# A spectral filter and a GEGLU block in one kernel: full rows in a product's last pass, signs moved from the filter to the row copies, shorter column steps

## The chip, the cores and the metric

The kernel runs on one core of a Trainium2 chip. It is measured by the device time of one execution in microseconds; the median over several executions counts, and less is better. The engines are TensorE (PE, with PEld for the loading of its weights), VectorE (DVE), ScalarE (ACT), GpSimd (POOL) and SyncE (SP). In this kernel GpSimd and SyncE do nearly nothing but issue DMAs.

## What is computed

Two branches work on the same 2048 x 576 input in fp32, and a sigmoid gate for each row mixes them:

```python
def reference(A_x, A_w_r, A_w_i, B_x, B_w_gate, B_w_up, B_w_down, gate_w):
    x = A_x                                              # [1, 2048, 576]
    g = sigmoid((x * gate_w).sum(-1, keepdims=True))
    a = irfft2(rfft2(x) * (A_w_r + 1j * A_w_i))          # spectral branch
    h = gelu(x @ B_w_gate) * (x @ B_w_up)                # 576 -> 4608
    b = h @ B_w_down                                     # 4608 -> 576
    return g * a + (1 - g) * b
```

## The kernel before

**GEGLU on TensorE.** An fp32 operand is split into a high and a low part that TensorE multiplies at its fast fp32 rate, and a product of two is the sum high x high, high x low, low x high. The 18 blocks of 256 hidden features are worked once for each half of 1024 rows. The first two blocks run plainly (`chain`); the other 34 turns are *products* (`products`, numbered from 0; product 16 is the first with the second half's rows). A product multiplies the first 512 input features in Strassen's manner: seven combinations of weights (`Block.prep`) by seven of the rows (named a11, a12, s2, s3, s1, a22, s4). `Block.seven` issues one such multiplication for 128 hidden features: six matmuls over 128 rows at L1367 and, at L1369, a last pass for the 64 remaining input features. Two sevens for each combination make 14 in a product. Behind them come the *downs* (12 matmuls at L966 in `down_mm`), whose result ScalarE scales into `stg` (L998) and GpSimd adds to the DRAM rows `yd` (`put`, L979, an accumulating DMA).

**The tails.** The 64 remaining features are worked in halves of 32. Their weights are made ready by `tail_piece`, ten pieces in all: load `wt` (L1245), form the seven combinations (`total`, L1249), take the high part, take the rest, and store them to `tails_d` in DRAM (L1263), as three groups of rows: high, high, low. Two pieces are handled during the plain blocks, eight in the first products, one every 12 gaps; all use the same buffer `wtb`. For every slot of weights `prep` then loads 96 rows of it (L1346, through SyncE). The row operand beside them, made by `tail_of`, has 128 rows: high, low, high, low; the last pass reads 96 of them.

**The spectral branch** runs between: the row transform on VectorE and ScalarE, the column transform, the product with the filter, and back. `columns` does the column transform for 16 blocks `kb` of frequencies; each takes two products of six matmuls on TensorE (L350) with matrices `col` (loaded by GpSimd, L336) and a pair of filter tiles `wf` (loaded by SyncE, L340). Frequencies past 288 are held as the conjugates of others, so the imaginary part of the filter takes a sign there (`sgn`, a multiplication at L439 for each block). `moved` copies the rows into the layout of the column stage and back, real parts on ScalarE, imaginary parts on VectorE (L570). At the end `adds` multiplies the spectral rows by the gate and GpSimd adds them to `yd` (L713). The last downs take the last eight blocks of rows from `yd` again (`load_last`, L1020, through SyncE), add theirs on VectorE (L1031) and write the output.

**What sets the order.** The program is written in one order, and each engine takes its instructions in that order. After each seven and each down stands a `gap()`: it runs functions that were put off by `at(n, fn)` to the n-th gap from there, and then lets the generator of the spectral branch go on for as long as `credit` lasts, which matmuls fill (`tick`) and work on VectorE uses up. A `yield None` in the generator ends the gap; `waits(n)` ends n. One block of `columns` takes 9 gaps at least (`STEP`).

**Between the halves.** The second half's operands are made in `other_operands` (called by `spectral`): ScalarE's copies (`highs`, through L234, the one line of all copies), VectorE's differences (`rests`, L1171, and `sums`, L1103), and stores to `kept` in DRAM. In product 15, the last of the first half, `swap` loads them into the operands (L1092 and L1093, on GpSimd's queue) as each becomes free: this is the *switch*, and the wait for the new operands falls in product 16. `forward` and `backward` are the butterflies over blocks of columns; `beside` runs them as a second generator next to the blocks.

Of the kernel before, what the change touches and what calls it, by code (L numbers as in the profile page):

```python
# [29 lines left out]
RATE = 1.08  # L30
STEP = 9
FIRST = 2
# [127 lines left out]
def _build(nc, tc, a):  # L160
    with ExitStack() as ctx:
# [34 lines left out]
        def set_tmp():  # L196
# [17 lines left out]
                for n in ("a11", "a12", "s2", "s3", "s1", "a22", "s4")}  # L214
        tails_d = [dram.tile([3 * P, 7 * 256], F32, name=f"tails{i}", tag=f"tails{i}") for i in range(len(PAIRS))]
        yd = [dram.tile([P, D], F32, name=f"yd{i}", tag=f"yd{i}") for i in range(NB)]
# [16 lines left out]
        def copy(o, i):  # L233
            act.activation(o, i, AF.Copy)  # L234
# [53 lines left out]
        def columns():  # L288
            G = [[rows[:, SW * (4 * i + j):SW * (4 * i + j + 1)] for j in range(4)] for i in range(2)]
            signs = rows[:, 8 * SW:8 * SW + KF]  # L290
            z, vs, w0 = (wtb[:, SW * i:SW * (i + 1)] for i in range(3))
            tmps = [free_low[:, SW * i:SW * (i + 1)] for i in range(2)]
            w1 = zb[0][:, 1664:1664 + SW]
            t0 = zb[0][:, 1664 + SW:1664 + SW + NK]
            turn = [d + 4 * q for d in range(4) for q in range(4)]
# [83 lines left out]

            def beside():  # L380
                yield from forward(1)
                for d in range(2):
                    yield from backward(d)
                    yield from forward(d + 2)
                for d in range(2, 4):
                    yield from backward(d)
# [7 lines left out]
            load_g(0)  # L394
            yield from waits(3)
            colm = mk("tmp", [2 * UNIT + 104], F32R)
# [7 lines left out]
            for c in range(2):  # L404
                load_ww(0, c)
            nc.sync.dma_start(signs, a["sgn"])
            at(2, lambda: load_g(1))
# [10 lines left out]
            for kb in range(16):  # L418
# [19 lines left out]
                vec.tensor_tensor(z, z, w0, ALU.mult)  # L438
                vec.tensor_tensor(two(w1)[:, :, 0:KF], two(w1)[:, :, 0:KF], signs[:, None, :].to_broadcast([P, 2, KF]), ALU.mult)  # L439
                yield from step(1.52)  # L440
                vec.tensor_tensor(vs, vs, w1, ALU.mult)
                vec.tensor_tensor(z, z, vs, ALU.add)
                yield from step(1.52)
                vec.tensor_tensor(vs2[:, 0], zr, zi, ALU.add)
# [12 lines left out]
                yield from waits(STEP - 9)  # L457
            copy(yh, vs)
# [105 lines left out]
        def moved(at, ts):  # L564

            for t in ts:
                for c in range(2):
                    o, i = at(t, c)
                    if c:
                        vec.tensor_copy(o, i)  # L570
# [578 lines left out]
        def other_operands():  # L1149
# [42 lines left out]

            yield from waits(4)
            load_xs(1, 2, quads[2])
# [46 lines left out]
        def tail_piece(n, raw_t=raw_t, high_t=high_t):  # L1241
# [17 lines left out]
            def store():  # L1259
                d = tails_d[n // 2].rearrange("(r p) (m c k) -> r p c m k", r=3, m=7, c=2)  # L1260
                w = 32 * len(PAIRS[n // 2])
                for r, x in enumerate((f(high_t), f(high_t), raw_t)):
                    nc.sync.dma_start(d[r, 0:w, n % 2], x[0:w])  # L1263
                stored[n // 2] = n % 2
# [3 lines left out]
        class Block:  # L1268
# [57 lines left out]
            def prep(self, k, m, lead=0):  # L1326
# [15 lines left out]
                def tail():  # L1342
                    n, q = self.tail_at[self.groups[k][1]]
                    assert stored[n]
                    d = tails_d[n].rearrange("(r q p) k -> q r p k", r=3, q=4)
                    nc.sync.dma_start(f(w[0:96, 512:768]), d[q, :, :, 256 * m:256 * (m + 1)])  # L1346

# [12 lines left out]
            def seven(self, ps, k, m, x, s, first, soon=None):  # L1360
# [3 lines left out]
                for t in range(2):  # L1364
                    hi, lo = (w[:, n + P * s:n + P * (s + 1)] for n in ((256, 0), (768, 1024))[t])
                    for q, (l, x) in enumerate(((hi, xh), (lo, xh), (hi, xl))):
                        pe.matmul(ps, l, x[:, t], start=first and t == 0 and q == 0, stop=False,  # L1367
                                  skip_group_check=True)
                pe.matmul(ps, w[0:96, 512 + P * s:512 + P * (s + 1)], xt[0:96], start=False, stop=True,  # L1369
                          skip_group_check=True)  # L1370
# [5 lines left out]
        def products(b, k):  # L1376
# [38 lines left out]
            for n, (name, nd) in enumerate(zip(("a11", "a12", "s2", "s3", "s1", "a22", "s4"), downs)):  # L1415
# [24 lines left out]
                for s in range(2):  # L1440
# [230 lines left out]
```

## Time and profile before

| | |
|---|---|
| runs | 1366.65, 1367.49 (median), 1371.56 us |
| profiled execution | 1365.51 us, of it the span 1363.4 us |
| mean granted TensorE clock | 0.991 |
| data moved by DMA | 262.71 MB, mean 193 GB/s |
| of it GpSimd's queue | 100.69 MB |
| of it SyncE's queue | 160.28 MB |

The chain of work that ended last is TensorE for 69%, DMA for 12%, issuing for 9%, ScalarE for 4%. Its largest parts by line are the downs (L966, 23%) and the sevens (L1367, 35%). Times in the rows below are microseconds from the span's start; a bracket behind a row gives the idle time of the engine before it and what ended it, and `x2` that two instructions of the same form follow each other. SPq and POOLq are the queues in which SyncE and GpSimd issue DMAs.

### The profile page before, as it was taken

The numbers are of one execution on the slowest core, as the hardware profiler recorded it, in microseconds if no ns is written. First come the engines' busy times: TensorE is split into PE (matmuls) and PEld (weight loads), VectorE is DVE, ScalarE is ACT, GpSimd is POOL, SyncE is SP. The second block draws the span as 40 slices with busy tenths as digits, with TensorE's granted clock in tenths as the row PEclk, the third lists the DMA queues.
The fourth block names the chain that finished last, engine by engine and source line by source line (L and its number), as shares of the span: only waits on it lengthen the run. The fifth ranks groups of instructions, "written<-read, shape, count | busy, mean of one in ns | idle before, by whom it ended". The sixth has DMA issues, their size and how long they took to land.

```text
span 1363.4 us, 20503 instructions
## 1 busy us (share of the span) xinstructions
PE 1322.1 (97%) x7210; PEld 1159.4 (85%) x7210; DVE 1137.4 (83%) x1750; ACT 841.8 (62%) x1419; POOL 283.7 (21%) x360
## 2 busy tenths in 40 slices
PE   9999999999999988999889999999999999999996
PEld 7888888888888877788778888888888888888896
DVE  8889889879999967587858778876899996799975
ACT  6665655666555656777557876766655656656551
POOL 0011211211221111224420122221221223222132
PEclk9999999999999999999989999999999999999999
DMA  9669998797767899979996698798877779867789
GB/s 350 211 159 218 198 228 188 166 248 143 134 134 136 193 295 257 240 160 269 329 220 174 174 245 174 156 215 188 168 134 137 133 135 201 199 124 132 128 181 233
DMA packets 165025, 262.71 MB, mean 193 GB/s; under 512 B 14394, under 2 KB 79226, under 8 KB 164026
## 3 DMA queue, kind: packets, MB, share of 16 engines
q0 software_dynamic: 50000, 100.69, 45.9%
q1 hardware_dynamic: 114490, 160.28, 36.6%
q8 instruction: 56, 0.92, 0.3%
q10 hardware_dynamic: 432, 0.44, 0.1%
q14 instruction: 47, 0.39, 0.1%
HBM read 140.64 MB, written 122.48 MB: 193 GB/s over the span
## 4 chain that ended last, share of the span: by engine, by line
PE 69%; DMA 12%; issue 9%; ACT 4%; DVE 3%; POOL 2%; SPq 0%; POOLq 0%; DVEq 0%; ACTq 0%
PE pdn L966 23%; PE pgu L1367 18%; PE px L1367 17%; PE pgu L1369 3%; PE px L1369 3%; POOL yd L979 2%; PE pdn L350 2%; DMA gub<-tails 2%; DMA kept_a<-tmp 2%; DMA slot<-tails 2%; DMA low<-ws 2%; DMA yd<-wtb 1%; DMA rows<-away 1%; ACT stg L998 1%; DMA tails<-wtb 1%
## 5 line engine op out<-in xcount | busy, mean ns | idle before, releaser
L979 POOL DMA_DIRECT2D yd<-stg x264 | 227.4, 864 | 998.3 <-ACT stg L998 871.1
L998 ACT ACTIVATE stg<-pdn,omg 128x576 f32<-128x576 f32 x276 | 204.6, 742 | 343.7 <-PE pdn L966 214.2
L966 PE MATMUL pdn<-dn,hb 128*128 128x288 f32 x1356 | 202.5, 296 | 3.0 <-ACT stg L998 2.7
L966 PEld LDWEIGHTS pdn<-dn,hb 128*128 128x128 f32 x1356 | 193.8, 189 | 12.7 <-ACT stg L998 3.9
L1367 PE MATMUL pgu<-xhi,gub 128*128 128x512 f32 x480 | 151.6, 397 | 4.3 <-ACT px L234 4.3
L966 PEld LDWEIGHTS pdn<-dn,ext 128*128 128x128 f32 x816 | 123.2, 189 | 15.0 <-DVE low L1031 4.8
L966 PE MATMUL pdn<-dn,ext 128*128 128x288 f32 x816 | 130.9, 296 | 4.4 <-DVE low L1031 4.4
L1367 PE MATMUL pgu<-til,gub 128*128 128x512 f32 x516 | 133.6, 394 | 1.4 <-ACT xraw L234 1.0
L966 PE MATMUL pdn<-dn,gub 128*128 128x288 f32 x816 | 129.3, 294 | 0.0
L234 ACT ACTIVATE gub<-low 128x512 fp32r<-128x512 f32 (+1 forms) x163 | 100.9, 620 | 32.0 <-DVE low L1339 26.3
L966 PEld LDWEIGHTS pdn<-dn,gub 128*128 128x128 f32 x816 | 115.3, 188 | 0.0
L1367 PE MATMUL px<-xhi,gub 128*128 128x512 f32 x344 | 109.3, 399 | 5.0 <-ACT pgu L234 3.4
L1354 DVE TENSOR_TENSOR gub<-low,gub 128x512 fp32r<-128x512 f32 x151 | 103.4, 685 | 11.3 <-ACT gub L234 11.3
L1367 PEld LDWEIGHTS pgu<-til,gub 128*128 128x128 f32 x516 | 94.3, 188 | 20.7 <-ACT xraw L234 1.6
L1367 PEld LDWEIGHTS pgu<-xhi,gub 128*128 128x128 f32 x480 | 87.2, 189 | 20.2 <-ACT px L234 4.7
L1367 PE MATMUL px<-til,gub 128*128 128x512 f32 x396 | 102.2, 393 | 0.0
L1367 PE MATMUL pgu<-xlo,gub 128*128 128x512 f32 x240 | 94.0, 391 | 0.0
L1367 PEld LDWEIGHTS px<-til,gub 128*128 128x128 f32 x396 | 72.6, 188 | 14.1
L1367 PEld LDWEIGHTS px<-xhi,gub 128*128 128x128 f32 x344 | 62.8, 190 | 17.3 <-ACT pgu L234 4.3
L966 PE MATMUL pdn<-dn,hx 128*128 128x288 f32 x444 | 70.3, 294 | 0.0
L1369 PE MATMUL pgu<-til,gub 96*128 96x512 f32 x172 | 67.9, 395 | 1.3 <-DMA gub<-tails 1.3
L1339 DVE TENSOR_TENSOR low<-low 128x512 f32<-128x512 f32 x98 | 67.4, 688 | 0.9
(303 smaller groups left out, 2728.9 us busy)
## 6 DMA issues: line engine op xcount, KB each, us to landing
yd<-stg POOLq DMA_DIRECT2D x264, 288.0 KB, 5.9
low<-ws SPq DMA_DIRECT2D x114, 256.0 KB
gub<-wd SPq DMA_DIRECT2D x68, 288.0 KB
gub<-tails SPq DMA_DIRECT2D x179, 96.0 KB
tails<-wtb SPq DMA_DIRECT2D x20, 448.0 KB
slot<-tails SPq DMA_DIRECT2D x59, 96.0 KB
gub<-ws SPq DMA_DIRECT2D x22, 256.0 KB
rows<-away SPq DMA_DIRECT2D x32, 145.0 KB
```

What stands on the lines that cost most here:

```text
L234: act.activation(o, i, AF.Copy)
L350: pe.matmul(v[:, al, :NK], cc[d][2 * al + q], two(x)[:, al], start=n == 0, stop=n == 2)
L966: pe.matmul(ps[half], h[:, l, c], d[:, q, half * HD:(half + 1) * HD], start=part == 0 and n == 0, stop=part == 1 and n == 2)
L979: pl.dma_start(yd[u], o, accum_op=ALU.add)
L998: at(n, lambda: put(u, lambda o: act.activation(o.rearrange("p (c k) -> p c k", c=2), v[:, :, 0:HD], AF.Copy, scale=omg[:, u:u + 1]), i == 0))
L1339: vec.tensor_tensor(o, p, q, ALU.subtract)
L1354: vec.tensor_tensor(v[:, 0:5:4], x, f(v[:, 1:4:2]), ALU.subtract)
L1367: pe.matmul(ps, l, x[:, t], start=first and t == 0 and q == 0, stop=False, skip_group_check=True)
L1369: pe.matmul(ps, w[0:96, 512 + P * s:512 + P * (s + 1)], xt[0:96], start=False, stop=True, skip_group_check=True)
```

## The change

Four edits:

- The last pass of a seven reads 128 rows. `tails_d` has a fourth group of rows, the low part again, which `tail_piece` stores too, and each load of tails brings 128 rows. So the product low x low is added for the last 64 features.
- The sign is taken out of the filter: `moved` multiplies the imaginary part by the sign in place of copying it (32 calls, on the way in and on the way back), L439's multiplication in each block goes, and the host's filter is no longer taken at the conjugates' places. `sgn` is loaded in `Block.open`, into a corner of a tile that held `t0`; `t0` moves to `rows`.
- A block of `columns` takes 8 gaps (`STEP`), with its VectorE work put together in fewer pieces; `columns` starts a gap sooner after its first loads, `other_operands` a gap later.
- The second butterfly, `forward(1)` in `beside`, waits until product 15 has begun its swaps (`ops["turn"]`).

```diff
@@ columns()
-            signs = rows[:, 8 * SW:8 * SW + KF]
-            t0 = zb[0][:, 1664 + SW:1664 + SW + NK]
+            t0 = rows[:, 8 * SW:8 * SW + NK]
...
             def beside():
+                while not ops.get("turn"):
+                    yield None
                 yield from forward(1)
...
             load_g(0)
-            yield from waits(3)
+            yield from waits(2)
...
-            nc.sync.dma_start(signs, a["sgn"])
...
                 vec.tensor_tensor(z, z, w0, ALU.mult)
-                vec.tensor_tensor(two(w1)[:, :, 0:KF], two(w1)[:, :, 0:KF], signs[:, None, :].to_broadcast([P, 2, KF]), ALU.mult)
+                vec.tensor_tensor(vs, vs, w1, ALU.mult)
                 yield from step(1.52)
-                vec.tensor_tensor(vs, vs, w1, ALU.mult)
+                if more:
+                    while made[0] < (kb + 1) // 4:
+                        yield None
+                    copy(xh, tile_of(kb + 1))
                 vec.tensor_tensor(z, z, vs, ALU.add)
-                yield from step(1.52)
                 vec.tensor_tensor(vs2[:, 0], zr, zi, ALU.add)
                 vec.tensor_tensor(vs2[:, 1], zr, zi, ALU.subtract)
                 at(1, lambda kb=kb: load_ww(kb + 1, 0))
                 at(2, lambda kb=kb: load_ww(kb + 1, 1))
-                yield from step(0.91)
-                if more:
-                    while made[0] < (kb + 1) // 4:
-                        yield None
-                    copy(xh, tile_of(kb + 1))
-                yield from step()
+                yield from step(1.67)
                 if more:
                     vec.tensor_tensor(xl, tile_of(kb + 1), f(xh), ALU.subtract)
                 yield from step(0.76)
-                yield from waits(STEP - 9)
+                yield from waits(STEP - 7)
@@ moved()
                     if c:
-                        vec.tensor_copy(o, i)
-                        yield 0.43
+                        vec.tensor_tensor(o, i, zb[0][:, 1664 + SW:1664 + SW + KF], ALU.mult)
+                        yield 0.45
@@ other_operands()
-            yield from waits(4)
+            yield from waits(5)
             load_xs(1, 2, quads[2])
             first = highs(A, 0)
@@ tail_piece()
-                for r, x in enumerate((f(high_t), f(high_t), raw_t)):
+                for r, x in enumerate((f(high_t), f(high_t), raw_t, raw_t)):
                     nc.sync.dma_start(d[r, 0:w, n % 2], x[0:w])
@@ Block.open()
+                nc.sync.dma_start(z[:, 1664 + SW:1664 + SW + KF], a["sgn"])
@@ Block.prep()
-                    nc.sync.dma_start(f(w[0:96, 512:768]), d[q, :, :, 256 * m:256 * (m + 1)])
+                    nc.sync.dma_start(f(w[:, 512:768]), d[q, :, :, 256 * m:256 * (m + 1)])
@@ Block.seven()
-                pe.matmul(ps, w[0:96, 512 + P * s:512 + P * (s + 1)], xt[0:96], start=False, stop=True,
+                pe.matmul(ps, w[:, 512 + P * s:512 + P * (s + 1)], xt, start=False, stop=True,
@@ products()
                 if turn:
+                    ops["turn"] = True
                     assert ops["kept"]
@@ host
-        wf[:, c, :, :, :, :KF] = w[np.where(k > 288, -kt % S, kt), np.minimum(k, D - k)][:, None]
+        wf[:, c, :, :, :, :KF] = w[kt, np.minimum(k, D - k)][:, None]
```

What the edits move is seen in the order in which the engines get their instructions; lines after the change are three lower past the edits. First ScalarE in product 12, at the start of `other_operands`, before. The copies out of `rows_94` are those of `highs`; `px0` and `px1` take the accumulators `pgu` over into others, after which TensorE may use them again; `slot` and `gub1_72` are weights of coming sevens, `stg2` a down's result, `hx` a hidden block.

```order
L234 ACTIVATE px0_4538<-pgu_4536 128x512
L234 ACTIVATE slot_74<-low_76 128x2x256
L234 ACTIVATE wtb_88<-rows_94 128x512
L234 ACTIVATE low_76<-rows_94 128x512 x2
L234 ACTIVATE xtl0_67<-rows_94 128x512
L234 ACTIVATE gub0_794<-rows_94 128x512
L234 ACTIVATE tmp_89<-rows_94 128x512 x2
L234 ACTIVATE px1_4539<-pgu_4537 128x512
L998 ACTIVATE stg2_86<-pdn_4573,omg_92 128x576
L234 ACTIVATE hx_127<-xraw_83 128x512
L234 ACTIVATE gub1_72<-low_76 128x2x256
```

The same place on ScalarE after the change:

```order
L234 ACTIVATE px0_4548<-pgu_4546 128x512
L234 ACTIVATE slot_74<-low_76 128x2x256
L234 ACTIVATE px1_4549<-pgu_4547 128x512
L995 ACTIVATE stg2_86<-pdn_4577,omg_92 128x576
L234 ACTIVATE hx_127<-xraw_83 128x512
L234 ACTIVATE wtb_88<-rows_94 128x512
L234 ACTIVATE low_76<-rows_94 128x512 x2
L234 ACTIVATE xtl0_67<-rows_94 128x512
L234 ACTIVATE gub0_796<-rows_94 128x512
L234 ACTIVATE tmp_89<-rows_94 128x512 x2
L234 ACTIVATE gub1_72<-low_76 128x2x256
```

The seven row copies have moved behind the second accumulator's copy, a down's result and a hidden block.

Second, GpSimd's queue in the switch, before. `til` and `xtl` hold operands that are swapped in from `kept_s`, `xtl_67<-col`, `tmp<-col` and `gub_73<-col` are the matrices of the next column products, and `yd` are sums of rows.

```order
L1092 DMA til_303<-kept_s_101 128x1024 x2
L1093 DMA til_303<-kept_s_101 128x512
L336 DMA xtl_67<-col 128x512
L979 DMA yd_116<-stg_85 128x576
L1092 DMA til_303<-kept_s_102 128x1024 x2
L1093 DMA til_302<-kept_s_102 128x512
L336 DMA tmp<-col 128x256
L336 DMA gub_73<-col 128x256
L979 DMA yd_117<-stg_86 128x576
```

And after:

```order
L1089 DMA til_303<-kept_s_101 128x1024 x2
L1090 DMA til_303<-kept_s_101 128x512
L976 DMA yd_116<-stg_85 128x576
L1089 DMA til_303<-kept_s_102 128x1024 x2
L1090 DMA til_302<-kept_s_102 128x512
L976 DMA yd_117<-stg_86 128x576
```

The three loads of `col` are gone from between these two swaps: the column products that they serve stand elsewhere, since the blocks of `columns` have another length and start.

Third, GpSimd's queue at the end of the program, before. `yd_119` to `yd_126` are the last eight blocks of rows; rows with `stg` are the last `put`s, the others the additions of the spectral rows (L713).

```order
L979 DMA yd_119<-stg_84 128x576
L979 DMA yd_120<-stg_85 128x576
L713 DMA yd_122<-wtb 128x576
L713 DMA yd_123<-wtb 128x576
L979 DMA yd_121<-stg_86 128x576
L713 DMA yd_124<-wtb 128x576
L979 DMA yd_122<-stg_87 128x576
L713 DMA yd_125<-low 128x576
L713 DMA yd_126<-low 128x576
L713 DMA yd_119<-tmp 128x576
L713 DMA yd_120<-tmp 128x576
L713 DMA yd_121<-tmp 128x576
```

And after:

```order
L976 DMA yd_126<-stg_87 128x576
L710 DMA yd_121<-low 128x576
L710 DMA yd_122<-low 128x576
L976 DMA yd_119<-stg_84 128x576
L710 DMA yd_123<-tmp 128x576
L976 DMA yd_120<-stg_85 128x576
L710 DMA yd_124<-tmp 128x576
L710 DMA yd_125<-tmp 128x576
L976 DMA yd_121<-stg_86 128x576
L976 DMA yd_122<-stg_87 128x576
```

The additions now stand ahead of the last `put`s. The column stage's last product stands 7 sevens earlier in the program than before. On SyncE's queue the stores of a piece of the tail weights, of 448 KB each, are four in place of three, ahead of the next piece's load.

More of the change, by code (lines that the diff above doesn't have):

```diff
@@ L30 @@
 RATE = 1.08
-STEP = 9
+STEP = 8
 FIRST = 2
@@ L214, in _build @@
                 for n in ("a11", "a12", "s2", "s3", "s1", "a22", "s4")}
-        tails_d = [dram.tile([3 * P, 7 * 256], F32, name=f"tails{i}", tag=f"tails{i}") for i in range(len(PAIRS))]
+        tails_d = [dram.tile([4 * P, 7 * 256], F32, name=f"tails{i}", tag=f"tails{i}") for i in range(len(PAIRS))]
         yd = [dram.tile([P, D], F32, name=f"yd{i}", tag=f"yd{i}") for i in range(NB)]
@@ L1259, in store @@
             def store():
-                d = tails_d[n // 2].rearrange("(r p) (m c k) -> r p c m k", r=3, m=7, c=2)
+                d = tails_d[n // 2].rearrange("(r p) (m c k) -> r p c m k", r=4, m=7, c=2)
                 w = 32 * len(PAIRS[n // 2])
-                for r, x in enumerate((f(high_t), f(high_t), raw_t)):
+                for r, x in enumerate((f(high_t), f(high_t), raw_t, raw_t)):
                     nc.sync.dma_start(d[r, 0:w, n % 2], x[0:w])
@@ L1344, in tail @@
                     assert stored[n]
-                    d = tails_d[n].rearrange("(r q p) k -> q r p k", r=3, q=4)
-                    nc.sync.dma_start(f(w[0:96, 512:768]), d[q, :, :, 256 * m:256 * (m + 1)])
+                    d = tails_d[n].rearrange("(r q p) k -> q r p k", r=4, q=4)
+                    nc.sync.dma_start(f(w[:, 512:768]), d[q, :, :, 256 * m:256 * (m + 1)])
                 v, x = (z.rearrange("p (b k) -> p b k", k=256) for z in (w, x))
```

## The prediction

> **What bounds the kernel now.** I read the page first: how much of the span TensorE is idle, and what a matmul costs there. The groups' columns are count, busy time and mean ns, and idle time before them.
>
> ```profile
> span 1363.4 us, 20503 instructions
> ## 1 busy us (share of the span) xinstructions
> PE 1322.1 (97%) x7210; PEld 1159.4 (85%) x7210; DVE 1137.4 (83%) x1750; ACT 841.8 (62%) x1419; POOL 283.7 (21%) x360
> ...
> L1367 PE MATMUL pgu<-til,gub 128*128 128x512 f32 x516 | 133.6, 394 | 1.4 <-ACT xraw L234 1.0
> ...
> L1369 PE MATMUL pgu<-til,gub 96*128 96x512 f32 x172 | 67.9, 395 | 1.3 <-DMA gub<-tails 1.3
> ```
>
> TensorE is busy in 97% of the span, and the change takes no matmul away. So it can gain only in TensorE's 41 us of gaps and in stretches of lower clock behind them. Second, I read windows: start and end, length, busy time of PE, PEld, DVE, ACT and POOL, granted clock, DMA share, GB/s.
>
> ```profile
> 440.00:480.00 40.00, 40.00 (x221) 35.24 (x220) 36.03 (x61) 26.71 (x45) 7.93 (x9) 1.00 0.81 193
> 480.00:520.00 40.00, 35.39 (x188) 30.43 (x187) 26.80 (x43) 21.36 (x38) 6.03 (x7) 0.96 1.01 292
> 520.00:560.00 40.00, 34.70 (x169) 29.32 (x168) 22.48 (x35) 30.07 (x52) 7.66 (x10) 0.91 0.94 256
> 504.00:508.00 4.00, 4.00 (x15) 3.32 (x16) 0.69 (x1) 1.44 (x3) 0.85 (x1) 0.63 0.86 264
> 540.00:545.00 5.00, 4.29 (x15) 3.67 (x16) 5.00 (x10) 5.00 (x10) 1.73 (x2) 0.66 0.72 173
> 685.00:690.00 5.00, 4.39 (x13) 3.85 (x14) 1.36 (x3) 1.83 (x4) 0.57 (x1) 0.50 0.61 140
> ```
>
> At 440 TensorE is full at clock 1.00: such a stage gives nothing. Around 500 and 540, while the second half's operands are prepared, and at 685, in the switch, it idles, and each stall is followed by a low clock. Third come TensorE's waits (sum, count, longest):
>
> ```profile
> PE px L1369 <- DMA slot<-tails: 7.1, 2, 6.9
> PE pgu L1367 <- ACT px L234: 6.1, 3, 4.3
> PE pdn L966 <- DVE low L1031: 4.6, 3, 2.7
> ```
>
> These three are the switch, the preparation and the end: the places that the change rearranges.
>
> **A. Preparation, product 12: -7.4.** ScalarE, then TensorE:
>
> ```profile
> 498.49 0.61 ACT L234 ACTIVATE wtb<-rows 128x512 fp32r<-128x512 f32 x1
> ...
> 503.17 0.58 ACT L234 ACTIVATE px<-pgu 128x512 f32<-128x512 f32 x1
> ```
>
> ```profile
> 503.80 1.22 PE L1367 MATMUL pgu<-xhi,gub 128*128 128x512 f32 x2 [4.28 <-ACT px L234]
> ...
> 525.44 0.73 PE L1367 MATMUL px<-xhi,gub 128*128 128x512 f32 x2 [1.62 <-ACT xraw L234]
> ```
>
> From 498.49 to 503.17 ScalarE makes seven copies of the second half's rows (one instruction form stands for two at two places), and the copy px<-pgu that frees TensorE's accumulator is behind them. TensorE waits 4.28 us and then runs 4 us at 0.63, which costs 4 x (1 - 0.63) = 1.48. The second burst costs 1.62 at 525.44. `other_operands` now starts a gap later, so both accumulator copies stand ahead of the first burst (order, above); the second burst falls behind the two xraw copies in the same way. That removes 4.28 + 1.48 + 1.62 = 7.4. What could be late next is VectorE:
>
> ```profile
> 511.82 0.69 DVE L1171 TENSOR_TENSOR wtb<-rows,tmp 128x512 fp32r<-128x512 f32 x1 [6.84 <-DMA kept_s<-wtb]
> ```
>
> It waits 6.84 us for a store of the rests and holds up the tail weights' work behind it. Today that cost TensorE nothing because it stood still itself; TensorE coming 5.8 us sooner eats most of that cover. If the wait eats all of the 5.8 (4.28 and 1.48), 1.6 are left: bounds -7.4 to -1.6. I take -7.4, since the waiting instruction also moves back by a gap.
>
> **B. Switch, product 16: -3.5.** SyncE's queue, TensorE, and the two DMA queues between 660 and 680 us (packets, MB, share):
>
> ```profile
> 663.41 0.72 SPq L1346 DMA_DIRECT2D slot<-tails  x1
> ```
>
> ```profile
> 685.61 0.77 PE L1369 MATMUL px<-til,slot 96*128 96x512 f32 x1 [6.86 <-DMA slot<-tails]
> ```
>
> ```profile
> q0 software_dynamic: 1898, 5.02, 81.9%
> q1 hardware_dynamic: 765, 1.36, 20.2%
> ```
>
> A tail issued at 663.41 isn't there 15 us later. In those 20 us q0 (GpSimd's: the swaps, `col`, the sums of rows) moves 5.02 MB and q1 (SyncE's) only 1.36: the tail is late because the swaps take the DMA engines. The stall is 6.86 us and the low clock after it 5 x (1 - 0.50) = 2.5, together 9.4. After the change the column step's three `col` loads, 256 + 128 + 128 KB, no longer stand between these swaps; at 5.02 MB in 20 us, 251 GB/s, 512 KB are 2.1 us. Against that, the five tails in flight carry 32 KB more each: 160 KB at q1's 68 GB/s are 2.4 us. The filter pair that stood among them is issued one tail sooner. Bounds: -9.4 (all of it goes) to +4 (the col loads fall beside the next swap, and the longer tails pay their 2.4 with some clock). I take -3.5, nearer the middle, because two of the three effects shorten the wait. On this queue's price the Trainium skill, "DMA: Bandwidth & Descriptors", section "Anatomy of one DMA — SWDGE (gpsimd) path", has a fit of about 2 us plus bytes over 436 GB/s; by it the 512 KB would move in an estimated 1.2 us, so B would be 0.9 less. The 251 GB/s of this window speak against it where the swaps crowd.
>
> **C. End: -3.5.** The wait for L1031 is 4.6 us in three places: the last downs add rows that came back from DRAM. GpSimd and SyncE:
>
> ```profile
> 1339.07 1.74 POOL L713 DMA_DIRECT2D yd<-tmp  x2 [0.22 <-issue]
> ```
>
> ```profile
> 1336.15 9.77 SPq L1020 DMA_DIRECT2D low<-yd  x4
> ```
>
> The four loads of yd take SyncE 9.77 us, since they follow the spectral rows' additions to yd, which are being issued up to 1339.07. With steps of 8 gaps the column stage's last product comes 7 sevens (some 18 us) earlier, and in the order five additions stand before the last four puts where three additions end the list today. Only a stall goes: -4.65 at best, 0 if the puts themselves, which stay, hold the loads. I take -3.5, for the additions are most of what is ahead of them.
>
> **D. Opening: +5.3.** Each prepared piece of the tail weights is stored a fourth time (448 KB), and the load of the next is behind that on SyncE:
>
> ```profile
> 168.74 3.81 SPq L1263 DMA_DIRECT2D tails<-wtb  x3
> ...
> 181.62 0.99 SPq L1245 DMA_DIRECT2D wtb<-wt  x2
> ```
>
> ```profile
> 188.97 1.64 PE L1367 MATMUL pgu<-til,gub 128*128 128x512 f32 x6 [1.00 <-ACT xraw L234]
> ```
>
> ```profile
> DVE wtb L1249 <- DMA wtb<-wt: 8.4, 4, 3.4
> ```
>
> ```profile
> DMA packets 4003, 3.70 MB, mean 246 GB/s; under 512 B 174, under 2 KB 3071, under 8 KB 4002
> ```
>
> The load overwrites what the stores read, so it waits for them: 181.62 - 168.74 = 12.9 us for three, at most 4.3 for a fourth. The last row is the window of these 15 us: at its 246 GB/s, 448 KB take 1.86. I take 1.86, as the stores of one piece overlap one another. VectorE waits for the load in four of eight pieces, 8.4 us in all. Of the longest, 3.4 at 186.60, 1.00 reached TensorE (188.97), so 2.4 are covered, and with that cover gone each further us counts. That piece pays 1.86; the other three have waits of 5.0 together, and 5.0 + 3 x 1.86 - 3 x 2.4 = 3.4. Sum 5.3. Bounds: 1.9 (that piece alone) to 17 (4 x 4.3). On SyncE's queue the fourth store also holds tail loads, by 3.81 / 3 = 1.3 us of issuing; they stand up to a gap ahead of need.
>
> **E. The rest: 0.** A matmul over 96 rows takes 395 ns and one over 128 takes 394, so the full last pass is free. The loads of tails grow from 96 to 128 KB: beside a full TensorE the stage at 440 has DMA to spare (193 GB/s, against 292 at 480); I bound this at 0 to +3, and take 0. On VectorE:
>
> ```profile
> L439 DVE TENSOR_TENSOR gub<-gub,rows 128x578 f32<-128x578 f32 x16 | 12.1, 755 | 1.2 <-DMA gub<-wf 1.2
> ...
> L444 DVE TENSOR_TENSOR wtb<-wtb 128x290 f32<-128x290 f32 x16 | 7.3, 455 | 0.0
> ...
> L570 DVE COPY tmp<-rows 128x289 f32<-128x289 f32 x8 | 3.7, 458 | 0.1
> ```
>
> Sixteen sign products (12.1 us) go, off the path: VectorE has 17% to spare. The copies that take over the signs become products of two tensors at 455 ns for 458: nothing. Here the Trainium skill ("VectorE: DVE Perf Modes", section "Mode 2×_2P — use both read ports for one tensor") says that a copy in SBUF may use both read ports, which an operation on two tensors can't; each of 32 copies would then become dearer by up to an estimated 0.23 us, 7 us hidden on VectorE. The rows disagree: this copy runs at the product's rate already. Shorter column steps press VectorE and ScalarE a little more per gap; stalls there are bounded at -6 to +4, taken as 0.
>
> **Sum.** -7.4 - 3.5 - 3.5 + 5.3 = -9.1. The profiled execution took 1365.51 us (the span and 2.1 around it), so 1356.4; the median of the runs, 1367.49, lies 2.0 higher, so **1358**.
>
> **Rivals.**
> - R1, the burst's wait is only replaced: TensorE arrives earlier at the work behind VectorE's 6.84 us wait and at the second burst, and A gives nothing: 1358 + 7.4, about 1366. For it: VectorE, waiting for a store, is in order. Against: that wait itself moves back a gap.
> - R2, the slower one: the fourth store stops TensorE in each of the eight pieces. At 4.3 us each, 34 in place of 5.3, the time is 1387. It decides for slower from 21 us on (14.4 gained elsewhere and 6.8 of the threshold), 2.7 a piece. For it: a piece already reaches TensorE. Against: four have no wait at all.
> - R3, more than forecast: all of B goes (9.4 for 3.5), product 13's stalls go with the burst (5.30 - 1.62 = 3.7 idle between 520 and 560, and 5 x (1 - 0.66) = 1.7 of clock), and D costs 1.9: 1358 - 5.9 - 5.4 - 3.4, about 1344. For it: all are crowding in the same place. Against: in 540 to 545 VectorE and ScalarE are full.
> - R4, the change doesn't do what it says: the column stage's shorter step is swallowed by waits for its loads or for the switch, which one butterfly now awaits, and it ends no earlier. Then C is 0: 1362.
>
> **How the numbers follow.** Forecast 0.50, R1 0.18, R2 0.10, R3 0.15, R4 0.07. A measurement of this kernel tells about 0.5%, 6.8 us, from no change: faster means under 1360.7. The forecast's own spread (1351 to 1364) lies below that for 0.42 of its 0.50; with 0.01 of R1, all 0.15 of R3 and 0.02 of R4, faster is 0.60, slower R2's 0.10, and 0.30 remain. The range, 1346 to 1370, holds the forecast, R1, R4 and nearly half of R3, 0.82. Its top is D at its 17 alone, or A at -1.6 with E at +3 and B at nothing; its foot is B at -9.4, D at 1.9, C whole and 1.5 us of the column stage's stalls.
>
> **What would show it.** A: px<-pgu ahead of the rows' copies, no 4.28 us wait near 500, clock near 1.0 in its window. B: the tail's wait in product 16 about half. C: the three waits for L1031's line under 1.5 us together, and the four loads far below 9.77. D: waits for wt near 14 us, four or five of them. E: 128-row passes at 395 ns. I am wrong if the wait for the kept stores takes A's place, if the wt wait passes 2.7 a piece, or if waits for gub<-tails, 1.3 us in all today, become several us.

## The result, and the profile after

| | before | after |
|---|---|---|
| median | 1368.38 us (7 runs, 1366.39 to 1371.56) | 1357.68 us (7 runs, 1357.06 to 1363.72) |
| profiled execution | 1365.51 us, span 1363.4 | 1358.51 us, span 1356.7 |

The ratio of the mean times is 0.9933, with a 95% interval of 0.9913 to 0.9953: 0.7% faster, 10.7 us between the medians. Between the two profiled executions it is less, 6.7 us of span, since the one of before is 2.9 us under its median and the one of after 0.8 us above. The forecast was 1358. But the sum came out by terms of which few had the size that the prediction gave them. To see this, the profiled span is cut at the products: from the end of one product's last pass to the end of the next one's, in us, and from the last of them to the end of the span.

| part | before | after | difference |
|---|---|---|---|
| start to the end of product 4 | 242.5 | 250.4 | +7.9 |
| products 5 to 11 | 247.4 | 245.1 | -2.3 |
| products 12 and 13 (preparation) | 89.1 | 85.5 | -3.6 |
| products 14 and 15 | 77.9 | 79.5 | +1.6 |
| product 16 (switch) | 49.4 | 48.8 | -0.6 |
| products 17 to 22 | 235.3 | 235.6 | +0.3 |
| products 23 to 32 | 355.3 | 352.7 | -2.7 |
| product 33 | 41.7 | 41.4 | -0.3 |
| from there to the end | 24.7 | 17.8 | -6.9 |

The ordinary product, where TensorE never waits, went from 35.34 to 35.01 us, 0.33 for each product, 11 us if each of the 34 gained it. The prediction had nothing there. First the page after, with the groups of the seven; then two groups of the page before that the prediction didn't show (count, busy us, mean ns, idle before):

```profile
span 1356.7 us, 20505 instructions
## 1 busy us (share of the span) xinstructions
PE 1315.2 (97%) x7210; PEld 1157.2 (85%) x7210; DVE 1134.2 (84%) x1734; ACT 842.2 (62%) x1419; POOL 285.0 (21%) x360
...
L1365 PE MATMUL pgu<-xhi,gub 128*128 128x512 f32 x480 | 150.3, 394 | 0.6 <-DVE gl L1391 0.4
L1365 PE MATMUL pgu<-til,gub 128*128 128x512 f32 x516 | 132.9, 392 | 2.7 <-ACT xraw L234 2.3
...
L1365 PE MATMUL px<-xhi,gub 128*128 128x512 f32 x344 | 107.7, 394 | 3.0 <-ACT pgu L234 3.0
```

```profile
L1367 PE MATMUL pgu<-xhi,gub 128*128 128x512 f32 x480 | 151.6, 397 | 4.3 <-ACT px L234 4.3
...
L1367 PE MATMUL px<-xhi,gub 128*128 128x512 f32 x344 | 109.3, 399 | 5.0 <-ACT pgu L234 3.4
```

The matmuls whose shape did not change became shorter: px<-xhi from 399 to 394 ns, pgu<-xhi from 397 to 394. TensorE's busy time fell by 6.9 us with the same 7210 matmuls. In the windows (same columns as in the prediction) it shows as more matmuls in a full stretch: 223 where 221 stood from 440 to 480.

```profile
440.00:480.00 40.00, 40.00 (x223) 35.41 (x222) 39.03 (x60) 27.08 (x47) 7.95 (x10) 1.00 0.79 174
480.00:520.00 40.00, 36.89 (x196) 32.10 (x195) 26.58 (x43) 23.56 (x41) 6.88 (x8) 0.96 1.00 292
520.00:560.00 40.00, 32.84 (x168) 27.34 (x167) 27.62 (x43) 27.00 (x47) 5.43 (x7) 0.96 0.98 272
512.00:516.00 4.00, 3.30 (x8) 2.63 (x9) 1.29 (x2) 1.20 (x3) 0.83 (x1) 0.60 0.91 234
...
689.00:694.00 5.00, 4.92 (x15) 4.21 (x16) 0.69 (x1) 1.72 (x3) 0.00 (x0) 0.53 0.65 170
172.00:176.00 4.00, 0.69 (x2) 0.60 (x3) 2.79 (x7) 1.44 (x2) 0.00 (x0) 0.86 0.94 204
176.00:180.00 4.00, 4.00 (x19) 3.43 (x18) 3.96 (x10) 1.26 (x2) 0.00 (x0) 0.71 0.75 224
```

The low clocks are still there, at 512 and 689, and there is a new one at 176, in the opening, where the kernel before has 1.00. TensorE's waits after:

```profile
PE pdn L963 <- ACT stg L995: 6.5, 7, 2.0
PE px L1367 <- DMA slot<-tails: 6.2, 1, 6.2
PE px L1367 <- DMA gub<-tails: 5.4, 3, 3.1
PE pgu L1367 <- DMA gub<-tails: 4.2, 1, 4.2
```

```profile
689.08 0.77 PE L1367 MATMUL px<-til,slot 128*128 128x512 f32 x1 [6.18 <-DMA slot<-tails]
```

The wait for px<-pgu (6.1 us) and that for the rows from yd (4.6 us) are gone from the top; the switch's, in the last row, is there as before; and two waits for gub<-tails have come, 3.1 in product 12 and 4.2 in product 2.

### The profile page after: what moved, and what is told of

It reads as the page before. It is cut to its first block, busy times and chain, and to the rows that moved or that the text cites. A ratio compares the mean times of both kernels' runs of the same rounds, so it can differ in the third digit from the quotient of the medians.

```text
span 1356.7 us, 20505 instructions
## 1 busy us (share of the span) xinstructions
PE 1315.2 (97%) x7210; PEld 1157.2 (85%) x7210; DVE 1134.2 (84%) x1734; ACT 842.2 (62%) x1419; POOL 285.0 (21%) x360
## 3 DMA queue, kind: packets, MB, share of 16 engines
q0 software_dynamic: 50000, 100.69, 44.5%
## 4 chain that ended last, share of the span: by engine, by line
PE 66%; DMA 13%; issue 9%; ACT 4%; DVE 4%; POOL 2%; SPq 1%; DVEq 0%; POOLq 0%; ACTq 0%
PE pdn L963 22%; PE pgu L1365 17%; PE px L1365 16%; PE pgu L1367 3%; PE px L1367 3%; DMA tails<-wtb 2%; DMA gub<-tails 2%; POOL yd L976 2%; PE pdn L349 2%; DMA slot<-tails 1%; DMA wtb<-wt 1%; DMA gub<-ws 1%; ACT til L234 1%; ACT stg L995 1%; DMA kept_a<-wtb 1%
## 5 line engine op out<-in xcount | busy, mean ns | idle before, releaser
L963 PEld LDWEIGHTS pdn<-dn,ext 128*128 128x128 f32 x816 | 123.7, 190 | 10.6 <-DVE low L1028 0.5
L1365 PE MATMUL px<-xlo,gub 128*128 128x512 f32 x172 | 67.6, 393 | 0.0
```

The source lines that it names most:

```text
L963: pe.matmul(ps[half], h[:, l, c], d[:, q, half * HD:(half + 1) * HD], start=part == 0 and n == 0, stop=part == 1 and n == 2)
```

## The experiments

Twelve kernels were run, and their profiled executions are cut in the same way. Each row is one execution, and those of one kernel differ by up to 12 us (before_zero: 1355.89 to 1367.44), so a difference of 1 or 2 us in one part says little. The ordinary product repeats to 0.01 us.

| kernel | to end of 4 | ordinary | 12, 13 | 14, 15 | 16 | 17 to 22 | last part |
|---|---|---|---|---|---|---|---|
| before | 242.5 | 35.34 | 89.1 | 77.9 | 49.4 | 235.3 | 24.7 |
| after | 250.4 | 35.01 | 85.5 | 79.5 | 48.8 | 235.6 | 17.8 |
| before_zero | 241.8 | 35.01 | 90.2 | 77.4 | 48.5 | 234.1 | 25.6 |
| before_128 | 248.2 | 35.01 | 89.4 | 77.5 | 50.2 | 233.7 | 24.1 |
| after_96 | 242.4 | 35.34 | 85.3 | 79.4 | 50.0 | 234.6 | 17.2 |
| after_zero | 244.4 | 35.01 | 84.6 | 79.0 | 48.5 | 235.6 | 17.5 |
| after_step9 | 248.6 | 35.01 | 85.9 | 80.4 | 50.6 | 230.5 | 25.3 |
| after_w4 | 249.3 | 35.01 | 90.6 | 77.7 | 53.8 | 234.9 | 17.6 |
| after_noturn | 251.3 | 35.01 | 85.7 | 90.0 | 49.6 | 234.9 | 17.2 |
| after_sgn | 250.6 | 35.01 | 86.2 | 79.8 | 49.6 | 237.1 | 25.2 |
| after_wtpool | 251.4 | 35.01 | 84.7 | 79.4 | 51.4 | 234.8 | 17.6 |
| after_nocol | 249.1 | 35.01 | 85.5 | 81.3 | 51.1 | 234.8 | 17.6 |
| zero_latewd | 243.0 | 35.01 | 85.1 | 79.4 | 47.8 | 237.2 | 18.5 |
| two_stores | 263.5 | 35.01 | 105.0 | 104.4 | 47.7 | 263.1 | 17.0 |

### The rows of the last pass

**before_zero** gives the kernel before a last pass over 128 rows and nothing else:

```diff
+                for s in self.slots:
+                    vec.memset(f(s[96:128, 512:768]), 0.0)
...
-                pe.matmul(ps, w[0:96, 512 + P * s:512 + P * (s + 1)], xt[0:96], start=False, stop=True,
+                pe.matmul(ps, w[:, 512 + P * s:512 + P * (s + 1)], xt, start=False, stop=True,
```

> Kernel before, but the last pass of a seven reads 128 rows, of which the last 32 of the weights are zeros set once; stores and loads of tails stay at 96 rows. Theory rows (a last pass over 96 rows slows the passes around it by some 22 ns a seven, which is what shortened the ordinary product from 35.34 to 35.03 us): ordinary product 35.0 us, 34 x 0.31 = 10.5 us off, about 1358. Rival schedule (the shorter products come from the other edits, or from the data of the fourth group): product 35.3 us, time about 1368.

Measured: 1361.13 us against 1365.28 for the kernel before, ratio 0.9958 (0.9940 to 0.9975), 5.7 us between the mean times; the profiled span is 1356.3, and the ordinary product 35.01 us. 32 rows of zeros, with no DMA and no instruction of the order changed but the four memsets, shorten the seven that they belong to. In products 6 to 10, from one pass's start to the next, the seven passes take on average 233, 235, 227, 231, 232, 227 and 230 ns in the kernel before, and 231, 229, 229, 229, 227, 227 and 227 here: five are shorter, the last pass itself among them. Why a pass over 96 rows does this is open. The time fell less than the 10.5 us that were expected: where TensorE waits for something else, a shorter pass only lengthens the wait. One group of the page:

```profile
L1369 PE MATMUL px<-xhi,gub 128*128 128x512 f32 x344 | 107.4, 393 | 6.4 <-ACT pgu L234 4.7
```

**before_128** is the kernel before with the first edit alone, and **after_96** the changed one without it (as in the first edit's lines of the diff, or back):

> Kernel before with the first edit alone (fourth group stored, 128 rows loaded and used). Theory rows, with the opening's loss put down to the fourth store: products 35.0 us, products 0 to 4 together about 9 us longer than that makes them, time 1368 - 10.5 + 9.4, about 1367, so no change to be seen. Rival schedule: products 35.3 us, opening the same 9 us longer, about 1378.

Measured: 1367.60 us against 1365.28, ratio 1.0011 (0.9995 to 1.0027). The ordinary product is 35.01, but products up to 4 end at 248.2, 6.4 later than in before_zero.

> Changed kernel with the first edit undone (three groups, 96 rows). Theory rows: products 35.3 us again (+10.5), the opening's 9.4 us gone, end still short: about 1358, and less by what the smaller tail loads give in products 12 to 22. In the middle, if the longer tail loads made the 3.1 us wait at 512.7, that wait is gone. Rival schedule: products stay at 35.0 us, about 1348.

Measured: 1358.73 us, ratio 0.9934 (0.9912 to 0.9956), the ordinary product 35.34 us again, the opening at 242.4. So the first edit gives up to 11 us in the passes and takes nearly all back, most of it in the opening (250.4 for 242.4): the whole change is as fast without it as with it (0.9933). The wait for tails in product 12 didn't go with the smaller loads: it is 2.65 us at 506.63.

**after_zero** takes the passes without the stores: three groups stored, 96 rows loaded, 32 rows of zeros (the memset of before_zero in the changed kernel).

> Changed kernel, three groups stored, 96 rows loaded, last pass over 128 rows with 32 rows of zeros set once. Theory rows: products 35.0 us without the opening's loss: 1357.7 - 9.4, about 1348, or a little less if smaller tail loads help in the middle; faster than both. Rival (the loss in the opening is from the other edits, such as the load of the signs in the opening): about 1357.

Measured: 1350.17 us, ratio 0.9872 (0.9851 to 0.9893). It is faster than both: 8.5 us less than after_96 by the ratios, and 8.3 less than the changed kernel.

### The opening

**after_wtpool** moves the loads of wt off SyncE's queue:

```diff
-                    nc.sync.dma_start(o, a["wt"][n // 2, n % 2, q].rearrange("p (b k) -> p b k", b=2))
+                    pl.dma_start(o, a["wt"][n // 2, n % 2, q].rearrange("p (b k) -> p b k", b=2))
```

> Changed kernel; the loads of wt go through GpSimd's queue, all else the same. If the opening's loss is a tail load on SyncE's queue that stands behind the wt load, which waits for four stores: the 4.2 us wait at 175 and its low clock go, products 0 to 4 end at about 243 in place of 250, about 1351. If it is the bytes (stores of 448 KB more, longer tail loads): no change, about 1358. If it is VectorE's wait for wt, as the prediction has it: no change either, with the waits of L1246 as long as now, 15.5 us.

Measured: 1358.88 us, ratio 0.9932 (0.9908 to 0.9956), the opening at 251.4: no gain. In the changed kernel SyncE's queue and TensorE show how the loss comes about:

```profile
152.51 8.21 SPq L1260 DMA_DIRECT2D tails<-wtb  x4
...
168.71 0.98 SPq L1242 DMA_DIRECT2D wtb<-wt  x2
169.79 0.56 SPq L1344 DMA_DIRECT2D gub<-tails  x1
```

```profile
175.31 0.79 PE L1367 MATMUL pgu<-xtl,gub 128*128 128x512 f32 x1 [4.19 <-DMA gub<-tails]
```

From the first of the four stores to the load of wt that waits for them 16.2 us pass (11.6 in the kernel before); the load of the next tail is behind that, issued at 169.79, 1.3 us ahead of its need, and comes 4.2 late, and the clock falls to 0.71. Product 2, in which this stands, takes 42.1 us in place of 35.3; it does so, with 41.4 to 42.3, in five of the seven kernels that store four groups and load wt on SyncE's queue, and in the other two product 3 takes 42.4 or more. With wt on the other queue this wait is gone, but VectorE, which waits for wt, then comes late in products 3 and 4. VectorE's waits for wt were 8.4 us in the kernel before and 15.5 in the changed one; here (sum, count, longest), and TensorE's waits for VectorE:

```profile
DVE wtb L1246 <- DMA wtb<-wt: 17.6, 6, 4.7
```

```profile
181.42 0.73 PE L1365 MATMUL px<-xhi,gub 128*128 128x512 f32 x2 [2.24 <-DVE gl L1391]
...
219.40 0.73 PE L1365 MATMUL pgu<-xhi,gub 128*128 128x512 f32 x2 [1.44 <-DVE gl L1391]
```

So the loss seems to move from one wait to the other: all pieces share one buffer, and the next load of wt has to wait for the fourth store too. Over the seven pieces that are followed by another in products 0 to 4, the time from the first store to the next load is 11.36 us on average before and 13.15 after.

**two_stores** was to take the third and fourth store away and keep the 128 rows: high and low are stored once, in interleaved rows, and the load reads the same 64 rows twice, by a step of zero; the row operand is laid out to fit (that part of the edit is left out below).

```diff
-                d = tails_d[n // 2].rearrange("(r p) (m c k) -> r p c m k", r=4, m=7, c=2)
+                d = tails_d[n // 2].rearrange("(p r) (m c k) -> r p c m k", r=2, m=7, c=2)
-                for r, x in enumerate((f(high_t), f(high_t), raw_t, raw_t)):
+                for r, x in enumerate((f(high_t), raw_t)):
...
-                    nc.sync.dma_start(f(w[:, 512:768]), d[q, :, :, 256 * m:256 * (m + 1)])
+                    nc.sync.dma_start(f(w[:, 512:768]), tails_d[n][None, 64 * q:64 * (q + 1), 256 * m:256 * (m + 1)].to_broadcast([2, 64, 256]))
```

> Changed kernel with a piece of the tail weights stored twice in place of four times (high, low, in interleaved rows), and each load of tails reading those 64 rows twice, so that it still brings 128 rows and 128 KB; the row operand is laid out to fit (high in its first 64 rows, low in the others). The computation is that of the changed kernel. If the fourth store makes the opening's loss: products 0 to 4 end at 244 or sooner (250.4 in the changed kernel, 244.4 with three stores and 96-row loads), about 1350 or less. If the longer loads of tails make it: they end at 248 to 251 as in the changed kernel, about 1357.

Measured: 1502.13 us, ratio 1.0989 (1.0969 to 1.1009). The expectation can't be read from it, for another cost covers it: TensorE waits 121 us for tails over the whole program (56.6 and 48.4 us for gub<-tails, 15.7 for slot<-tails). The windows of DMA (busy share in tenths, then GB/s, in 40 slices from 320 to 355 us) show such loads:

```profile
DMA  1111111999616996114799718971117995988999
GB/s 60 48 50 53 51 49 47 383 382 387 228 49 100 302 219 142 32 29 84 270 109 177 155 40 104 169 152 47 28 31 92 145 207 106 315 287 156 222 225 284
```

From 320 to 326 us, where tail loads are nearly all that runs, some two of the 16 DMA engines are busy (SyncE's queue takes 13.6% of the 16), at some 50 GB/s. How the loss in the opening divides between the fourth store and the longer loads is therefore not shown by a kernel of its own.

### The end

**after_step9** has `STEP = 9` in the changed kernel.

> Changed kernel with blocks of the column stage of 9 gaps again. If the end's gain (24.7 us from the last seven to the end before, 17.8 after) comes from the earlier end of the column stage: the stalls on the rows loaded from yd return, some 5 to 7 us, about 1363 to 1365. If it came from the other edits (start of the stage, the moved butterfly): 17 to 18 us from the last seven to the end, about 1358.

Measured: 1363.47 us, ratio 0.9981 (0.9964 to 0.9998), 25.3 us from the last seven to the end. The waits for the rows from yd are back, 4.78 and 1.53 us, where the changed kernel has one of 0.28, and its four loads of yd take 5.31 us:

```profile
1344.24 1.81 PE L963 MATMUL pdn<-dn,ext 128*128 128x288 f32 x6 [4.78 <-DVE low L1028]
...
1348.88 1.06 PE L963 MATMUL pdn<-dn,ext 128*128 128x288 f32 x6 [1.53 <-DVE low L1028]
```

```profile
1342.38 1.06 PE L963 MATMUL pdn<-dn,ext 128*128 128x288 f32 x6 [0.28 <-DVE low L1028]
```

```profile
1333.73 5.31 SPq L1017 DMA_DIRECT2D low<-yd  x4
```

The time behind the last matmul, 4.4 us, stays as in the changed kernel (4.5), where the kernel before has 6.4: that part does not come from the step.

**after_sgn** puts the sign back on the filter, in the host's data too, with the rest of the change:

```diff
+                sgn = zb[0][:, 1664 + SW:1664 + SW + KF]
+                vec.tensor_tensor(two(w1)[:, :, 0:KF], two(w1)[:, :, 0:KF], sgn[:, None, :].to_broadcast([P, 2, KF]), ALU.mult)
                 vec.tensor_tensor(vs, vs, w1, ALU.mult)
-                yield from step(1.52)
+                yield from step(2.28)
...
-                        vec.tensor_tensor(o, i, zb[0][:, 1664 + SW:1664 + SW + KF], ALU.mult)
+                        vec.tensor_copy(o, i)
...
```

> Changed kernel with the signs on the filter again: a multiplication of 0.75 us for each of the 16 blocks on VectorE, and plain copies of the imaginary parts in place of 32 products. By the prediction (both hidden on VectorE): about 1358, ordinary products 35.0 us and the row copies at 0.45 us in either form. If the signs matter: products 14 to 22 longer by some of the 12 us, about 1362 or more.

Measured: 1365.53 us, ratio 0.9998 (0.9983 to 1.0012), 25.2 us at the end. The expectation of 1358 was wrong. The multiplication is hidden on VectorE, but it counts against the credit that lets the generator go on, and so a block takes longer in the program: the last column product stands behind 22.7 products' worth of sevens, near the 22.6 of the kernel before, where in the changed kernel it is 22.1. The short step gives its gain only together with the sign's move. The wait:

```profile
1351.03 1.81 PE L965 MATMUL pdn<-dn,ext 128*128 128x288 f32 x6 [6.13 <-DVE low L1030]
```

### The preparation

**after_w4** has `waits(4)` again in `other_operands`.

> Changed kernel with other_operands starting a gap earlier, as before. If the later start is what took the 4.3 us wait for px<-pgu away: that wait and its low clock are back in product 12 and the tail wait of 3 us there goes, product 12 about 43.9 less 0.3 (against 41.8), +2 us, about 1360. If the order of ScalarE's copies didn't matter: product 12 stays at 41.8 and the time at 1358.

Measured: 1367.15 us, ratio 0.9999 (0.9981 to 1.0017). The wait for px<-pgu is back, products 12 and 13 take 90.6 us against 85.5, and more than was expected goes in the switch, where the tail comes 10.59 us late and product 16 takes 53.8:

```profile
512.48 1.22 PE L1365 MATMUL pgu<-xhi,gub 128*128 128x512 f32 x2 [4.75 <-ACT px L234]
...
699.83 0.77 PE L1367 MATMUL px<-til,slot 128*128 128x512 f32 x1 [10.59 <-DMA slot<-tails]
```

Another 3.7 us stand in product 6, ahead of the edit, at a tail load that comes 1.81 late; why, no run shows. In the changed kernel ScalarE, SyncE and TensorE show what came in place of the burst:

```profile
503.24 0.58 ACT L234 ACTIVATE px<-pgu 128x512 f32<-128x512 f32 x1
...
505.05 0.62 ACT L234 ACTIVATE wtb<-rows 128x512 fp32r<-128x512 f32 x1
```

```profile
502.38 0.54 SPq L1344 DMA_DIRECT2D gub<-tails  x1
```

```profile
512.70 0.69 PE L1367 MATMUL px<-til,gub 128*128 128x512 f32 x1 [3.11 <-DMA gub<-tails]
```

The copies of rows start behind px<-pgu, as the order said. But the tail that is needed 7 us later was issued at 502.38, behind the loads of xs and six stores to kept on SyncE's queue. Its wait and the clock of 0.60 behind it, 3.1 and 4 x (1 - 0.60) = 1.6 us, take more than half of the 7.4 that were forecast.

### The switch

**after_nocol** issues no load of col in products 15 and 16, so the column products there work with old matrices and the spectral branch is not computed:

```diff
-                if kb < 16:
+                if kb < 16 and ops.get("k") not in (15, 16):
                     for q, o in cc_parts[s]:
...
```

> Changed kernel without any load of col that falls in products 15 and 16 (nine loads, 2.3 MB; the column products there work with matrices of an earlier block, so the spectral branch is not computed). If col loads on GpSimd's queue beside the swaps make the tail late, as the prediction has it, the 6.2 us wait in product 16 falls by 2 us or more, and the time to about 1353 to 1356. If the swaps themselves and the order on SyncE's queue make it: the wait stays at 5.5 to 7 us and the time within 1 us of the changed kernel's.

Measured: 1360.06 us, ratio 0.9939 (0.9917 to 0.9961). The wait in product 16 is 6.88 us: 2.1 MB less on GpSimd's queue (98.59 for 100.69 in the whole program) do nothing for it.

```profile
691.88 0.77 PE L1367 MATMUL px<-til,slot 128*128 128x512 f32 x1 [6.88 <-DMA slot<-tails]
```

**zero_latewd** works on the other queue, with after_zero as its base:

```diff
-                if n == 0 and k:
+                if n == (2 if k == 16 else 0) and k:
                     b.load_d(k)
```

> Kernel after_zero, with product 16's load of wd (576 KB) issued two combinations later on SyncE's queue, behind the tail that comes late there (and not ahead of it). If what the tail waits for is the data ahead of it on its own queue, which the swaps leave about 68 GB/s: the 5.9 us wait in product 16 shrinks to under 2 us and product 16 from 48.5 to about 42, about 1343. If it is the swaps alone: the wait stays at 5 to 7 us, about 1350.

Measured: 1350.11 us, ratio 0.9889 (0.9872 to 0.9905), the same as after_zero. The one wait of 5.90 us became two:

```profile
678.13 0.47 PE L1369 MATMUL px<-til,slot 128*128 128x512 f32 x1 [2.86 <-DMA gub<-col]
...
686.49 0.47 PE L1369 MATMUL pgu<-til,gub 128*128 128x512 f32 x1 [2.49 <-DMA gub<-tails]
```

For the first the profile names a load of col as what ended it; the matmul itself reads `til` and `slot`. Neither theory holds as it was put. The order on SyncE's queue decides which load is late, but 5.3 to 5.9 us are waited in all.

**after_noturn** takes the butterfly's wait for the switch away.

> Changed kernel without the second butterfly's wait for the switch. If the moved butterfly has a part in the end's gain or in products 12 to 16: the time from the last seven to the end goes above 20 us, or products 12 to 16 (213.8 us together) change by over 2 us. If it only moves VectorE's work: 17 to 18 us at the end, about 1358.

Measured: 1367.84 us, ratio 1.0018 (1.0005 to 1.0031). The end stays at 17.2, but products 14 and 15 take 90.0 us for 79.5. There is one more column product in them, and the butterfly's work falls among ordinary sevens; the longest wait in them is for a load of col behind the first swaps:

```profile
664.82 1.79 PE L349 MATMUL pdn<-tmp,xtl 128*128 128x290 f32 x6 [4.15 <-DMA xtl<-col]
```

So this edit is worth 10 us beside the others, and the prediction gave it no term.

## Why the prediction came out, point by point

**E, the step that failed: "so the full last pass is free".** Taken at 0, it was -11 us in the passes (34 x 0.33), the largest term of the change. Of this the time kept 5.7 us in before_zero against before and 8.5 in after_zero against after_96, by the ratios. The step compared the durations of the two kinds of last pass, 395 and 394 ns, as if a pass cost the same whatever stands around it. What the runs show is that in a seven that ends with 96 rows other passes are up to 6 ns longer. A sign of it was on the page: px<-xhi at 399 ns beside pgu<-til at 394.

**D, the opening: right in kind, somewhat small.** Taken at +5.3 with bounds of 1.9 to 17, it was 7.2 us (before_128 against before_zero) and 8.3 (the changed kernel against after_zero) by the ratios, of which 6.4 and 6.0 stand in the opening of the traces. The mean price of a fourth store, 13.15 - 11.36 = 1.8 us from store to load, is near the 1.86 of the prediction, and VectorE's waits for wt came to 15.5 us where it expected some 14. What it put aside, "they stand up to a gap ahead of need", decided: the late one was a tail load on SyncE's queue behind the wt load, in one piece with 16.2 us. after_wtpool shows that, with this wait gone, VectorE's wait for wt reaches TensorE in its place. The prediction's own sign of being wrong, waits for gub<-tails of several us, came: 5.4 and 4.2 us. It put today's at 1.3; the kernel before has another 1.2 at px.

**A, the preparation: the mechanism right, half the size.** Taken at -7.4, products 12 and 13 gave -3.6, of it 0.7 from E; with 96 rows in both kernels (after_96 against before) it is -3.9. The wait for px<-pgu went as the order said, and after_w4 brings it back. The prediction named the 6.84 us wait on VectorE as what could be late next. That wait is still 7.0 us, but what TensorE waited for was another, a tail load on SyncE's queue behind the stores to kept.

**B, the switch: wrong.** Taken at -3.5, product 16 gave -0.6, of it 0.3 from E, and with 96 rows in both kernels +0.6. The step "512 KB are 2.1 us" counted col loads that were issued at 642 to 652 us, 11 us and more ahead of the late tail; the three behind it, at 665 to 675, are still there after the change, at 668 to 677, and after_nocol shows that without any of them the wait is no shorter. What the wait is made of is open: it kept its 5 to 7 us with 96 and 128 rows, with and without col, rose to 10.6 in after_w4, and was divided, not shortened, by another order.

**C, the end: the mechanism right, too small.** Taken at -3.5 and bounded at -4.65, it was -6.9. The waits fell from 4.65 to 0.28, as bounded; the rest is 1.9 us behind the last matmul, where the last store of the output is issued 0.6 us behind it in both kernels but the span ends sooner, and some in the downs around the waits. after_step9 shows the step's length at work in the waits, and after_sgn that the sign's move belongs to it. The prediction had that move at nothing. Where the 1.9 us come from no run shows.

**The sum.** That 1358 came out is luck. after_96, the change without its first edit, gains 9.0 us by the ratio, where A, B and C were put at 14.4; and the first edit, put at +5.3, costs nothing that can be seen (0.9933 with it, 0.9934 without). Two errors of some 5 us have cancelled: E, left out, paid for D, and this made up for what A and B did not give. The second butterfly's wait, worth 10 us beside the others, had no term at all.

**A rule put aside.** The prediction weighed the Trainium skill's "VectorE: DVE Perf Modes", section "Mode 2×_2P — use both read ports for one tensor", and held the rows against it: 455 ns for a product, 458 for a copy. But these rows differ in more than the number of tensors: L444's reads and writes plain rows, and `moved` reads or writes every eighth element. Where both are plain, the kernel before has the difference that the rule lets one expect:

```profile
L492 DVE TENSOR_TENSOR tmp<-rows 128x512 f32<-128x512 f32 x16 | 11.0, 688 | 0.2
...
L490 DVE TENSOR_SCALAR tmp<-rows 128x512 f32<-128x512 f32 x8 | 3.2, 421 | 0.0
```

L492 works on two tensors, L490 on one. The products that came read as the copies did:

```profile
L567 DVE TENSOR_TENSOR tmp<-rows,gub 128x289 f32<-128x289 f32 x8 | 5.9, 735 | 0.1
```

735 ns are 0.28 us more than the copy; the prediction's estimate from the page was up to 0.23. So the trace agrees with the rule, and the step of eight, which makes the copy as slow as a plain product, had hidden it. The cost, 14.5 us for the 32 copies and 23.0 for the products, is hidden, as was said: products 5 to 11, in which half of them stand, are as short as in before_zero, which has copies there (245.1 us).

## What to carry to other kernels

Compare the durations of passes that the change does not touch: where the same shape has two durations in one profile, its neighbours may be the cause. Before a wait is booked as a gain, look on every queue for the transfer that is needed next in the same place, not only at the engine that waited beside it. Where a generator advances by a credit, work that is hidden on its engine still sets how soon the stage ends.

## What the runs showed that was not expected

- A 96-row pass among 128-row passes: px<-xhi takes 399 ns beside it and 393 to 394 without it, the product 35.34 and 35.01 us, also where the added rows hold zeros. Why is open.
- A load of 128 rows that reads 64 rows twice, with an outer step of zero, ran at some 50 GB/s with some two of the 16 DMA engines busy, and the kernel took 144 us more than the changed one.
- A multiplication of two tensors with one operand read in steps of eight took 735 ns for 289 elements; an operation on two tensors with plain rows took 455 ns for 290. A copy in steps of eight took 458 ns for 289, an operation on one tensor with plain rows 421 for 512.
